# Ten short products from a 128x64 tile of ones in place of five wide ones from a 128x384 region, at the start of an attention and feed-forward kernel

## Chip, core and metric

The kernel runs on one core of a Trainium2 chip. The metric is the device time of one execution in microseconds; the kernel before takes 919.75 us, the median of 10 runs that lie between 919.09 and 921.16 us.

## What is computed

The reference has two blocks. In the first, queries and keys of 32 heads (4 batches of 8, 768 positions, 64 numbers each) are hashed: the sign of six projections gives each position a bucket, and attention counts only keys in the query's own bucket. The second block is a feed-forward layer over 3072 tokens with a gate of erf and softplus.

```python
q_bits = (np.einsum('bhsd,dk->bhsk', q, proj) > 0).astype(np.int64)
k_bits = (np.einsum('bhsd,dk->bhsk', k, proj) > 0).astype(np.int64)
mask = q_bucket[:, :, :, None] == k_bucket[:, :, None, :]
scores = np.where(mask, scale * np.matmul(q, k.transpose(0, 1, 3, 2)), -1e9)
attn = softmax(scores)          # over the keys
x = attn @ v                    # laid out as 3072 tokens x 512
h = x @ w_in                    # 512 -> 2048
out = (h * erf(softplus(h))) @ w_out
```

Nothing that the change touches enters the output: the products it edits multiply ones by ones, and no instruction reads their results.

## The kernel before

All matmuls are on float32 data, except those that carry the mask, which are bfloat16. A float32 matmul stands in the profile as two MATMUL instructions ("passes" below), each with its own weight load (LDWEIGHTS, the row PEld).

**Attention.** The 32 heads are worked as 16 pairs; the two heads of a pair sit in partitions 0 to 63 and 64 to 127. `fetch` loads one pair: queries and keys transposed to 128x768, and the values. For pair 0 it is called with `quick=True`: queries and keys come in two halves of 384 columns. The first halves go out first, q from SP's queue and k from ACT's queue; then SP's queue sends the second halves, k before q, and then the values. Each load is two DMAs, one for each head.

For pair 0 the bits are made by a short sequence that is written out by hand, ahead of the planned order:

1. the constant products (L779 to L786), which are the subject of the change;
2. for each half in turn, `hash_bits` (L369): two matmuls 128x64 by 128x384, q into partitions 0 to 63 and k into 64 to 127 of one PSUM tile (so the passes for q and for k run side by side);
3. `take_bits` (L409) for that half: `sign_bits` on ACT (L386), `spread_bits` twice on DVE (L397), `double_bits` on DVE (L407). They fill the tile `both`, from which the mask is multiplied.

`hash_bits` reads `proj_sb`, which DVE fills from a small DMA (`proj_in`, L251, copies L255).

Everything after this is put in order by `arrange` (L118), which plans with costs written in the kernel: each engine gets its instructions in the planned order. The plan does not contain the constant products or the bits of pair 0. It begins on PE with two `plain` score products (q by k, without mask, `st<-q,k`, L550), then `score` adds the mask part (`st<-both`, L550), ACT takes the exponential (L568), DVE adds the exponentials up (`sum_keys`, L619), and `weigh` multiplies them by the values (`av`, L631). The bits of every later pair go a longer way: `bits_of` on PE (L812), sign on ACT (L821), one multiplication on DVE (L831), out to DRAM from POOL's queue (`bd<-sg`, L841), and back into `both` from POOL's queue (`both<-bd`, L850). For pair 1 this happens while pair 0 is being scored. SP's queue fetches the inputs of the next pairs; POOL's queue fetches feed-forward weights (`raw`), which ACT and DVE convert beside the attention.

**Feed-forward.** Seven products in place of eight for each block of 2x2 (sums made by DVE ahead of and behind them), in stages with the erf gate on ACT and DVE between two sets of products.

**The names that matter here.** `ones` is a constant tile 128x64, filled by DVE at L247; it serves the row sums of the attention later (`divisor`, L666). `w_sum` is a large tile that the feed-forward fills much later; before, its first 384 columns are filled with ones at L248 and serve as `warm`. `bank("...")` (L299) takes a tile of 128x512 from a PSUM pool with a single buffer: each call is a new tile in the same place.

```python
    WARM = 5
    nc.vector.memset(ones, 1.0)
    nc.vector.memset(w_sum[:, 0, 0, 0:HS], 1.0)
    warm = w_sum[:, 0, 0, 0:HS]
```

Of the kernel before, what the change touches and what calls it, by code (L numbers as in the profile page):

```python
# [63 lines left out]
P = 128  # L64
# [129 lines left out]
def kernel(  # L194
# [11 lines left out]
    nc = tc.nc  # L206
    B, H, S, D = v.shape
# [5 lines left out]
    HS = S // 2  # L213
# [15 lines left out]
    small = ctx.enter_context(tc.tile_pool(name="small", bufs=3))  # L229
    QR = 32  # L230
    QB = QR // 2
    WARM = 5
    proj_sb = const.tile([P, 2 * QR], F32, name="proj_sb")
    weight = const.tile([P, 2], F32, name="weight")
    proj_q = const.tile([P, QR], F32, name="proj_q")
# [1 line left out]
    ones = const.tile([P, D], F32, name="ones")  # L237
# [5 lines left out]
    w_sum = const.tile([P, 3, 2, FH], F32, name="w_sum")  # L243
# [1 line left out]
    blocks = []  # L245
    stats = const.tile([P, 2, NPAIR, 2], F32, name="stats")
    nc.vector.memset(ones, 1.0)  # L247
    nc.vector.memset(w_sum[:, 0, 0, 0:HS], 1.0)  # L248
    warm = w_sum[:, 0, 0, 0:HS]
    proj_in = const.tile([P, 2 * NBIT], F32, name="proj_in")  # L250
    nc.gpsimd.dma_start(out=proj_in, in_=proj2)  # L251
    nc.vector.memset(proj_sb, 0.0)
    for ab in range(2):
        rows = slice(ab * D, ab * D + D)
        nc.vector.tensor_copy(  # L255
            out=proj_sb[rows, ab * QR : ab * QR + NBIT],
# [5 lines left out]
    for c, (end, factor) in enumerate(  # L262
# [12 lines left out]
            out=steps[:, c : c + 1],  # L275
# [9 lines left out]
    for ab in range(2):  # L285
        rows = slice(ab * D, ab * D + D)
        nc.vector.tensor_copy(
            out=proj_q[rows, ab * QB : ab * QB + NBIT],
# [10 lines left out]
    def bank(name):  # L299
        return misc.tile([P, 512], F32, name=name, tag="bank")  # L300
# [45 lines left out]
    def fetch(i, load, quick=False):  # L346
        d = dict(
            q=load.tile([P, S], F32, name="q", tag="q"),
            k=load.tile([P, S], F32, name="k", tag="k"),
            v=load.tile([P, NC, P], F32, name="v", tag="v"),  # L350
        )
        b, j = divmod(i, JP)
        parts = ((0, "q"), (0, "k"), (1, "k"), (1, "q")) if quick else ((None, "q"), (None, "k"))
        for half, what in parts:
            cols = slice(0, S) if half is None else slice(half * HS, half * HS + HS)
            queue = nc.scalar if quick and what == "k" and half == 0 else nc.sync
            for ab in range(2):
                queue.dma_start(  # L358
                    out=d[what][ab * D : ab * D + D, cols],
                    in_=qkT[2 * i + ab, "qk".index(what) * D : "qk".index(what) * D + D, cols],  # L360
                )
        for ab in range(2):
            nc.sync.dma_start(  # L363
                out=d["v"][:, :, ab * D : ab * D + D],
                in_=v[b, 2 * j + ab].rearrange("(c p) d -> p c d", p=P),
            )
        return d
# [48 lines left out]
    def attention():  # L416
        NS = NPAIR * 4
        with (
# [357 lines left out]
                pairs[i] = fetch(i, load)  # L776

            pairs[0] = fetch(0, load, quick=True)
            for n in range(WARM):  # L779
                nc.tensor.matmul(  # L780
                    out=bank("warm")[:, 0 : 2 * P],
                    lhsT=warm[:, 0:P],
                    rhs=warm[:, P:HS],
                    start=True,
                    stop=True,
                )  # L786
# [917 lines left out]
    with tc.manual_schedule():  # L1704
        late = attention()
        feed_forward(judge, late)
# [57 lines left out]
```

## Time and profile before

| what | us |
|---|---|
| median of 10 runs | 919.75 |
| the profiled execution, its own time | 920.35 |
| its span in the trace | 918.5 |
| PE busy | 905.5 |
| DVE busy | 819.2 |
| ACT busy | 768.1 |
| ones filled by DVE (L247), start and duration | 0.82, 0.11 |
| w_sum filled by DVE (L248), start and duration | 0.96, 0.38 |
| first constant product, start | 1.39 |
| first pass of the bits of pair 0, start | 7.66 |
| first mask product of pair 0, start | 12.57 |
| first exponential, start | 12.96 |

The profiled execution's own time is 1.85 us more than its span, and 0.6 us more than the median of the runs. "Busy" of PE counts a pass from its start to its modelled end, and passes overlap in the pipeline, so a row's duration is longer than the distance from one pass to the next. In the timeline a line gives start, duration, engine, line of code, operation and tile, and at its end the idle time before it with what ended that. In an answer about one tile, the three numbers after the count are the shortest, median and longest duration in nanoseconds.

### The profile page before, as it was taken

Reading aid. Unit: us, or ns where it says so; the run is one execution under the profiler, and the core shown is the slowest. Engines: PE = TensorE matmul, PEld = TensorE weight load, DVE = VectorE, ACT = ScalarE, POOL = GpSimd, SP = SyncE. Lnnn points to the kernel's source line nnn. Section 1 sums busy time; section 2 is a strip of 40 time slices with the busy share of each in tenths; the row PEclk is TensorE's granted clock in tenths of the full one; section 3 lists DMA queues with packets and bytes.
Section 4 is the critical chain, followed back from the end, with each engine's and each line's share of the span. In section 5 each row is a group of like instructions: output and inputs, shape, how many; then the busy total and the mean of one; then the engine's idle time right before and its main releaser. Section 6 shows DMA issues by size and latency. Waiting matters only on the chain.

```text
span 918.5 us, 13120 instructions
## 1 busy us (share of the span) xinstructions
PE 905.5 (99%) x5006; PEld 659.2 (72%) x5006; DVE 819.2 (89%) x1020; ACT 768.1 (84%) x1002; POOL 46.8 (5%) x83
## 2 busy tenths in 40 slices
PE   9999999999999999999999999999999999999996
PEld 4444444444444478888888888888888888888885
DVE  4899999999899979899999799998999889988995
ACT  5888887788887749999988998899989988899891
POOL 1211111111111000000000000000000000000000
PEclk9999999999999999999999999999999999999998
DMA  8455576655673131102022012211221120011211
GB/s 205 118 154 160 157 185 192 184 150 154 177 197 108 59 121 64 46 9 95 12 74 76 35 46 72 78 35 46 70 81 35 35 81 35 35 35 46 69 35 49
DMA packets 62966, 83.05 MB, mean 90 GB/s; under 512 B 34174, under 2 KB 47342, under 8 KB 62896
## 3 DMA queue, kind: packets, MB, share of 16 engines
q1 hardware_dynamic: 56672, 64.08, 24.0%
q0 software_dynamic: 6064, 17.86, 6.0%
q8 instruction: 41, 0.67, 0.3%
q14 instruction: 29, 0.24, 0.1%
q10 hardware_dynamic: 160, 0.20, 0.1%
HBM read 64.71 MB, written 17.40 MB: 89 GB/s over the span
## 4 chain that ended last, share of the span: by engine, by line
PE 93%; DVE 2%; DMA 2%; SPq 1%; ACT 1%; issue 0%; POOL 0%; DVEq 0%; POOLq 0%; ACTq 0%
PE M L1323 31%; PE X L1183 28%; PE st L550 16%; PE av L631 13%; PE M L1183 3%; PE z_ps L666 1%; PE bits L812 1%; SPq L358 1%; DMA v<-in_v_dram 1%; DMA raw<-in_w_in_dram 1%; DVE e L1237 0%; DVE h L1265 0%; SPq L363 0%; DMA both<-bd 0%; DVE S L1280 0%
## 5 line engine op out<-in xcount | busy, mean ns | idle before, releaser
L1250 DVE SCALAR_TENSOR_TENSOR e<-w,e 128x1024 f32<-128x1024 f32 x144 | 173.3, 1219 | 5.8 <-ACT w L1246 3.0
L568 ACT ACTIVATE e_all<-st 128x768 f32<-128x768 f32 x192 | 151.2, 813 | 14.0 <-PE st L550 13.9
L1246 ACT ACTIVATE w<-w,cq 128x1024 f32<-128x1024 f32 x144 | 160.6, 1143 | 1.9
L550 PE MATMUL st<-q,k 64*128 64x384 f32 x768 | 156.0, 485 | 0.0
L1323 PE MATMUL M<-w_out_sb,h 128*128 128x256 f32 x576 | 140.2, 379 | 0.4 <-DVE h L1265 0.4
L631 PE MATMUL av<-e_all,v 128*64 128x385 f32 (+1 forms) x768 | 131.1, 490 | 0.0
L1183 PE MATMUL X<-x,w_in_sb 128*128 128x256 f32 x512 | 121.1, 379 | 0.0
L1323 PEld LDWEIGHTS M<-w_out_sb,h 128*128 128x128 f32 x576 | 109.3, 190 | 15.9 <-DVE h L1265 1.1
L1183 PEld LDWEIGHTS X<-x,w_in_sb 128*128 128x128 f32 x512 | 97.0, 190 | 13.8 <-ACT h L1201 0.6
L631 PEld LDWEIGHTS av<-e_all,v 128*64 128x64 f32 x768 | 52.3, 136 | 67.5 <-issue 65.7
L550 PEld LDWEIGHTS st<-q,k 64*128 64x128 f32 x768 | 68.7, 189 | 35.6 <-issue 34.9
L1323 PE MATMUL M<-wt,S 128*128 128x256 f32 x384 | 93.4, 379 | 0.4 <-DVE S L1280 0.4
L1183 PE MATMUL X<-x_sum,w_sum 128*128 128x256 f32 x344 | 81.7, 380 | 1.8 <-ACT h L1201 1.8
L1323 PEld LDWEIGHTS M<-wt,S 128*128 128x128 f32 x384 | 72.9, 190 | 10.7 <-DVE S L1280 0.8
L1183 PEld LDWEIGHTS X<-x_sum,w_sum 128*128 128x128 f32 x344 | 65.0, 190 | 12.0 <-ACT h L1201 3.3
L1201 ACT COPY h<-X 128x512 f32<-128x512 f32 x85 | 49.1, 577 | 22.3 <-PE X L1183 21.4
L1227 DVE SCALAR_TENSOR_TENSOR w<-w,e 128x1024 f32<-128x1024 f32 x48 | 58.4, 1220 | 9.7 <-ACT w L1222 9.7
L550 PE MATMUL st<-both 64*128 64x384 bf16 x384 | 63.2, 324 | 0.5 <-DMA both<-bd 0.3
L1265 DVE TENSOR_TENSOR h<-h,e 128x1024 f32<-128x1024 f32 x48 | 58.0, 1220 | 5.8 <-ACT e L1261 5.5
L1241 ACT ACTIVATE w<-e 128x1024 f32<-128x1024 f32 x48 | 50.4, 1050 | 13.2 <-DVE e L1237 13.0
L1237 DVE TENSOR_TENSOR e<-e,w 128x1024 f32<-128x1024 f32 x48 | 57.4, 1217 | 2.7 <-ACT e L1233 2.6
L1205 DVE TENSOR_TENSOR h<-X,h 128x512 f32<-128x512 f32 x65 | 44.8, 689 | 16.4 <-PE X L1183 15.4
(133 smaller groups left out, 1377.6 us busy)
## 6 DMA issues: line engine op xcount, KB each, us to landing
wt<-wt SPq DMA_DIRECT2D x24, 768.0 KB, 4.3
raw<-in_w_out_dram POOLq DMA_DIRECT2D x16, 512.0 KB, 4.0
raw<-in_w_in_dram POOLq DMA_DIRECT2D x14, 512.0 KB, 4.3
v<-in_v_dram SPq DMA_DIRECT2D x32, 192.0 KB, 4.8
xs<-x SPq DMA_DIRECT2D x16, 384.0 KB, 2.6
q<-in_qkT_dram SPq DMA_DIRECT2D x30, 192.0 KB, 4.3
k<-in_qkT_dram SPq DMA_DIRECT2D x30, 192.0 KB, 4.9
r<-rd SPq DMA_DIRECT2D x30, 192.0 KB, 3.4
```

Source lines behind the costliest of these rows:

```text
L550: nc.tensor.matmul(out=st[:, ab, 0:HS], lhsT=d["k" + src][rows, keys], rhs=d["q" + src][rows, cols], start=(part == 0), stop=(part == 1),)
L568: nc.scalar.activation(out=e[:, :, 0:HS], in_=st[:, :, 0:HS], func=AF.Exp, scale=scale)
L631: nc.tensor.matmul(out=d["av"][rows, 0:w], lhsT=d["v"][:, g * GC + c, rows], rhs=e[:, ab, 0:w], start=(g == 0 and c == 0), stop=(g == 1 an ...
L1183: nc.tensor.matmul(out=d[where][:, u, :], lhsT=a[:, kc, f : f + P], rhs=b[:, kc, :], start=(first and u == 0 and kc == 0), stop=(last and ...
L1201: nc.scalar.copy(out=quarter(p, q), in_=st[p][where])
L1227: nc.vector.scalar_tensor_tensor(out=w, in0=w, scalar=-1.0, in1=st[p]["e", v], op0=ALU.add, op1=ALU.subtract)
L1237: nc.vector.tensor_tensor(out=s, in0=s, in1=st[p].pop(("w", v)), op=ALU.subtract)
L1241: nc.scalar.activation(out=z, in_=st[p]["s", v], func=AF.Square)
L1246: nc.scalar.activation(out=q, in_=z, func=AF.Square, bias=cq[:, j : j + 1])
L1250: nc.vector.scalar_tensor_tensor(out=s, in0=st[p].pop(("q", v, j)), scalar=ERF_Q[j][1], in1=s, op0=ALU.add, op1=ALU.mult,)
L1265: nc.vector.tensor_tensor(out=h, in0=h, in1=st[p].pop(("s", v)), op=ALU.mult)
L1323: nc.tensor.matmul(out=banks[name][:, sub, :], lhsT=a[:, u, sub * P : (sub + 1) * P], rhs=b[:, u, :], start=(c == 0 and k == 0), stop=(c = ...
```

## The change

The products go from five to ten. Each one now has a stationary operand of 64 columns (`ones` itself) and a moving operand of 128 columns, which is one column of `ones` read 128 times over (a step of zero), where it had 128 and 256. They write 64 partitions by 128 columns in place of 128 by 256. The PSUM tile is taken once, ahead of the loop, and all ten write to the same place in it; before, each of the five took a new tile. The fill of 384 columns of `w_sum` goes; the products wait for the fill of `ones` (64 columns), which stands first on DVE in both versions.

```diff
-    WARM = 5
+    WARM = 10
...
     nc.vector.memset(ones, 1.0)
-    nc.vector.memset(w_sum[:, 0, 0, 0:HS], 1.0)
-    warm = w_sum[:, 0, 0, 0:HS]
...
             pairs[0] = fetch(0, load, quick=True)
+            warm = bank("warm")
             for n in range(WARM):
                 nc.tensor.matmul(
-                    out=bank("warm")[:, 0 : 2 * P],
-                    lhsT=warm[:, 0:P],
-                    rhs=warm[:, P:HS],
+                    out=warm[0:D, 0:P],
+                    lhsT=ones,
+                    rhs=ones[:, 0:1].broadcast_to([P, P]),
                     start=True,
                     stop=True,
                 )
```

## Prediction

> **What bounds the kernel now.** First the page: busy times, then the chain that ended last.
>
> ```profile
> PE 905.5 (99%) x5006; PEld 659.2 (72%) x5006; DVE 819.2 (89%) x1020; ACT 768.1 (84%) x1002; POOL 46.8 (5%) x83
> ...
> PE 93%; DVE 2%; DMA 2%; SPq 1%; ACT 1%; issue 0%; POOL 0%; DVEq 0%; POOLq 0%; ACTq 0%
> ```
>
> PE is busy throughout and carries the chain. What comes earlier in the first 13 us therefore comes off the end, unless PE later waits for something that has not moved. The edit lies wholly in this stretch, so next the timeline of its start:
>
> ```profile
> 0.82 0.11 DVE L247 MEMSET ones<- 128x64 f32 x1 [0.82 <-PEq L1744]
> 0.96 0.38 DVE L248 MEMSET w_sum<- 128x384 f32 x1
> ...
> 1.39 0.50 PEld L780 LDWEIGHTS warm<-w_sum 128*128 128x128 f32 x2 [1.39 <-DVE w_sum L248]
> ...
> 2.67 0.50 PEld L780 LDWEIGHTS warm<-w_sum 128*128 128x128 f32 x2 [0.78 <-PE warm L780]
> ...
> 4.02 0.35 DVE L255 COPY proj_sb<-proj_in 64x6 f32<-64x6 f32 x2 [2.49 <-DMA proj_in<-in_proj_dram]
> ...
> 7.66 0.90 PE L373 MATMUL bits<-q,proj_sb 128*64 128x384 f32 x1
> ...
> 8.36 0.85 PE L373 MATMUL bits<-q,proj_sb 128*64 128x384 f32 x1
> ...
> 9.64 0.85 PE L373 MATMUL bits<-q,proj_sb 128*64 128x384 f32 x1
> ...
> 10.57 0.58 ACT L386 ACTIVATE both<-bits,sgn 128x384 bf16<-128x384 f32 x1 [0.70 <-PE bits L373]
> ...
> 12.57 0.65 PE L550 MATMUL st<-both 64*128 64x384 bf16 x6
> ```
>
> Each of the five products starts 1.28 us after the last; its weight load waits for the product before (0.78 us idle each time), because each takes the one PSUM buffer anew. Only at 7.66 do the bits begin, though their inputs were there: `proj_sb` at 4.37 (4.02 + 0.35), the first halves of q and k at 4.98 (the trace's last landing). So the products themselves hold up the kernel.
>
> The answer for tile `bits` shows the second thing, PE's clock:
>
> ```profile
> L373 PE MATMUL bits<-q,proj_sb x4: 847/847/903, 7.7 to 9.6; 128*64 128x384 f32 x4
> ...
> L812 PE MATMUL bits<-q,proj_q x4: 486/498/510, 18.8 to 19.1; 128*32 128x384 f32 x4
> ```
>
> Passes over the same 384 columns take 847 ns at 8 us and 498 at 19; start to start they are 0.64 us apart in L373 (9.64 - 9.00) and, in the attention's `av` rows, 0.32. So PE runs at half speed at first. (The granted clock in the view by stretches reads 1.00 there, but nothing is recorded before the first change.) In the single records two score passes are 0.64 apart until 11.87 and the next 0.38: full speed came at about 12.0, that is 4.3 us after the unbroken work began at 7.66. Six us of spaced products, which stream 0.85 of every 1.28 us (67%), had not brought it.
>
> **The change part by part.**
>
> *The fill removed.* The products wait for `ones`, filled at 0.93, not for `w_sum`, filled at 1.34. With the 0.05 us between fill and first load (1.39 - 1.34) they start at 0.99: 0.40 earlier. The other early DVE work gains nothing, since the copies wait for `proj_in` until 4.02. The first reuse of the PSUM bank (`z_ps`, 29.8) comes long after.
>
> *The products.* At half speed a pass of 128 columns takes 0.64 x 128/384 = 0.213 us. A 64-column weight load costs 0.06 when it stands exposed (8.36 - 7.66 - 0.64). Ten products are 20 passes: 0.99 + 0.06 + 20 x 0.213 = 5.31. The trace does not show such a pass. Below, full speed would halve it, but the bits then wait for inputs until 5.0. Above, each weight load stays exposed: 20 x 0.27 = 5.5, end 6.5. I take the lower pass cost: at 12.89 a weight load of 187 ns under a pass of 0.16 delayed the next pass by nothing. The broadcast read has no row either; from no loss (as any column read) to twice the pass (8.5 us, end 9.6). I take no loss, as the `av` rows read their 385 columns at the same pace as the score rows their 384, whatever the source.
>
> The Trainium skill speaks against short passes ("TensorE: Matmul & The Clock Gate", "Back-to-back issue gap"): with its weight load a 128-column matmul costs 81 ns where the stream alone takes 56. By that ratio the products would end at 7.2 and about 0.8 us of the gain below would go.
>
> *The waits removed.* One tile for all ten products means no turn of the buffer. Score products already write one PSUM tile repeatedly on PE with no wait (L550's waits name exponentials and DMAs, none PE).
>
> *The first half of the bits* starts at 5.3 in place of 7.66. Next late is the second half's q: its last load is issued at 4.20 and lands at 6.75; PE takes four waits 0.13 apart, so q starts about 6.9 and k 7.05. Had that cover not been there, 0.3 us more would be won.
>
> *The clock.* Dense work from 0.99 and 4.3 us more gives full speed at 5.3, if these half-wide products count as the bits did. Then the first half takes 0.06 + 2 x 0.32 = 0.70 and hides before 6.9; the second ends at 7.05 + 0.70 = 7.75, before 10.29 (9.65 + 0.64). ACT follows 0.28 later (10.57 - 10.29), at 8.03; from there to the mask's weights it was 12.25 - 10.57 = 1.68 through ACT and DVE: 9.71, first mask product 9.75. The plain scores (four passes of 0.32, ending about 9.3) hide beneath; before, at half speed, they ended at 12.57 and set that time. The front moves 12.57 - 9.75 = 2.8 us.
>
> By the Trainium skill (same page, "The HAM clock gate") the gate opens at the end of the first fully busy window of 3.4 us that runs freely. That gives an estimate of 4.4 to 7.9 for the release; at the late end about 0.3 us of the 2.8 goes. This trace's one release, 4.3 us after dense work began, fits.
>
> *What has not moved.* Pair 1's mask goes out and back through DRAM:
>
> ```profile
> PEld L550 <- DMA both<-bd: 0.6, 1, 0.6
> ```
>
> PE already waits 0.6 us for it at 26.65. The store `bd<-sg`, issued at 21.21, lands in 1.9 us with DMA nearly idle (share 0.12 from 20 to 25). Moved 2.8 earlier it meets pair 2's loads (share 1.2 from 18 to 20), whose issue by SP depends on nothing that moved. The next such store, at 31.57 among traffic, took 3.1. So the loss lies between 0 and 1.2 us and goes wholly into PE's wait. I take 0.6: the 3.1 row also had a weight load ahead of it in POOL's own queue, which the moved one has not. Otherwise PE, ACT and DVE move together; pair 1's loads land by 13.5, before their use.
>
> **Sum.** 2.8 - 0.6 = 2.2 us: 920.35 becomes 918.15 for the profiled execution. It lies 0.6 above the median of the runs, so the median becomes 917.55; I say **917.5**.
>
> **Rivals.**
>
> A, the forecast: dense products bring full speed before the second half of the bits. 916.3 to 918.3 (loss 0 to 1.2, clock a little late).
>
> B: products that fill 64 of 128 columns do not count, and the clock comes 4.3 us after the bits begin, or after their short gap at 6.9. The second half then ends at 7.05 + 0.06 + 1.28 = 8.39, the plain scores run at half speed until 9.6 or beyond, and the mask product starts at 10.45 to 11.25: 1.3 to 2.1 won, 0.4 given back: 918.0 to 918.9, or 918.4. For it: the row's 64 columns use half the array. Against: nothing here shows what the clock counts; the bits' 64-column passes came as side-by-side pairs.
>
> C, slower than before: the framework keeps a wait between products that overwrite one tile. Each costs what L780's row shows around its passes, 1.28 - 0.16 - 0.85 = 0.27, plus 0.06 and 2 x 0.213: 0.75. The tenth starts at 0.99 + 9 x 0.75 = 7.74, the bits at 8.4 (+0.06 + 0.43 + 0.15): 0.7 later than 7.66, 920.4. It decides once a product costs over 0.67 us ((7.66 - 0.99)/10). For it: DVE and ACT rows do wait for their own engine; against: L550 on PE does not.
>
> D: the early start is used up later, in waits for DMA that stays in place: 919.7. For it, the 0.6 wait above; against, PE's 99%, and few PE waits after 30 us.
>
> **Chances.** A 0.55, B 0.25, C 0.08, D 0.08, worse mishaps (such as the doubled pass) 0.04. About 0.2%, or 1.84 us, is what a measurement of this kernel can tell from no change, so faster means under 917.91. A lies there four times in five (0.44) and B one in five (0.05): faster 0.49. Slower by as much needs over 921.59: the mishaps and a bad C or D, 0.06. Within: 0.45. The range, 916.2 to 919.9, takes in A, B and D and leaves out C.
>
> **What would show it.** Right: products from about 0.99, 0.21 us from pass to pass, none waiting for PE; bits from about 5.3, the second half at 6.9, its passes near 500 ns rather than 847; the first mask product near 9.75; PE's wait for `both<-bd` grown from 0.6 to about 1.2. B: 847 ns in all bits rows. C: 0.75 us between products with waits named PE. D: the first exponential 2 to 3 us earlier and the last matmul not. The forecast fails first if short passes cost more than 0.29 us, since the products then outlast the second half's landing.

## The result and the profile after

| what | before | after |
|---|---|---|
| median, us (runs) | 919.47 (28) | 923.58 (8), from 922.36 to 924.71 |
| ratio, 95% interval | | 1.0042 [1.0033, 1.0051] |
| the profiled execution, us | 920.35 | 922.51 |
| its span, us | 918.5 | 920.7 |

The change makes the kernel 0.42% slower, by about 4 us, where 2.2 us were forecast as won. (The kernel before was run again beside it; hence 919.47 and not 919.75.) The profiled execution is 2.16 us longer than that of before.

The page first: busy times, the granted clock (PEclk, how much of its full speed TensorE's clock was allowed, in tenths) in 40 slices, and the chain that ended last.

```profile
PE 904.9 (98%) x5016; PEld 661.6 (72%) x5016; DVE 819.2 (89%) x1019; ACT 767.8 (83%) x1002; POOL 46.5 (5%) x83
...
PEclk9899999999999999999999999999999999999999
...
PE 95%; DVE 2%; DMA 1%; ACT 1%; SPq 0%; issue 0%; POOL 0%; DVEq 0%; ACTq 0%; POOLq 0%
```

PE still carries the end, and it is busy 0.6 us less in a span that is 2.2 us longer. So it waits more. The 8 in the second slice (23 to 46 us) is new (before, only the last slice has an 8): the clock was lower there for a while.

The timeline of the start shows the front as it was meant to be:

```profile
0.99 4.42 PE L779 MATMUL warm<-ones 128*64 128x128 f32 x20 [0.99 <-DVE ones L247]
...
5.24 0.49 PE L371 MATMUL bits<-q,proj_sb 128*64 128x384 f32 x1
...
6.74 0.51 PE L371 MATMUL bits<-q,proj_sb 128*64 128x384 f32 x1 [0.62 <-DMA q<-in_qkT_dram]
...
9.02 0.65 PE L548 MATMUL st<-both 64*128 64x384 bf16 x6
...
17.66 0.54 POOL L840 DMA_DIRECT2D bd<-sg  x1 [13.81 <-DVE sg L830]
```

Products at 0.99 without a wait, bits at 5.24, their second half behind its load at 6.74, and the first mask product at 9.02 where it was at 12.57: 3.55 us earlier. The store `bd<-sg` follows at 17.66, also 3.55 earlier (21.21 before). Thus far everything moved together. The waits from 18 to 32 us (engine, line, what was waited for, then the sum, how often, the longest) show where it stops:

```profile
ACT e_all L566 <- PE st L548: 5.9, 3, 4.9
POOL both L849 <- DMA bd<-sg: 5.1, 1, 5.1
...
PE st L548 <- DMA both<-bd: 4.0, 2, 3.5
```

The same two rows before:

```profile
POOL both L850 <- DMA bd<-sg: 2.0, 1, 2.0
...
PE st L550 <- DMA both<-bd: 0.3, 1, 0.3
```

POOL waits 5.1 us for the store (2.0 before), and PE 4.0 us for the loads back (0.3 before). The timeline of that place:

```profile
22.75 1.11 SPq L356 DMA_DIRECT2D q<-in_qkT_dram  x2
...
23.29 1.14 POOL L849 DMA_DIRECT2D both<-bd  x2 [5.08 <-DMA bd<-sg]
...
26.19 0.48 PE L548 MATMUL st<-both 64*128 64x384 bf16 x1 [3.54 <-DMA both<-bd]
...
27.12 0.50 PE L548 MATMUL st<-both 64*128 64x384 bf16 x1 [0.46 <-DMA both<-bd]
...
28.88 1.62 PE L548 MATMUL st<-q,k 64*128 64x384 f32 x4
```

The row of before for the second mask product of pair 1:

```profile
26.66 0.33 PE L550 MATMUL st<-both 64*128 64x384 bf16 x1 [0.30 <-DMA both<-bd]
```

The store lands at 22.61 (23.12 before): of 3.55 us, 0.5 is left. The loads back go out at 23.29, beside pair 3's loads, which SP's queue now sends at 22.75 (26.29 before). The second lands after 3.21 us (2.24 before), and the second mask product of pair 1 runs at 27.12, 0.46 us later than before. And the passes behind it take 1.62 us for four, where they take 0.81 elsewhere. The view by stretches tells why (busy time and instructions of PE, PEld, DVE, ACT, POOL; then granted clock, DMA share, GB/s):

```profile
22.00:24.00 2.00, 0.64 (x4) 0.03 (x2) 1.97 (x3) 2.00 (x3) 0.71 (x2) 1.00 0.00 1
24.00:26.00 2.00, 0.00 (x0) 0.00 (x0) 1.97 (x3) 0.06 (x1) 2.00 (x3) 0.91 0.94 255
26.00:28.00 2.00, 1.35 (x5) 0.81 (x7) 1.33 (x2) 0.00 (x0) 0.32 (x1) 0.50 1.03 229
28.00:30.00 2.00, 2.00 (x10) 1.27 (x8) 0.00 (x0) 0.81 (x1) 0.00 (x0) 0.50 0.50 193
30.00:32.00 2.00, 2.00 (x8) 0.79 (x4) 0.00 (x0) 0.81 (x1) 0.00 (x0) 0.50 0.00 0
32.00:34.00 2.00, 2.00 (x21) 0.78 (x22) 0.24 (x1) 1.66 (x4) 0.00 (x0) 0.88 0.00 0
```

PE idles from 22.64 to 26.19, the granted clock falls to half at 25.65, and it stays there until 32.47, while PE, from 27.12 without a pause, works on pair 1's scores. The first `av` of pair 1 starts at 33.33 instead of 30.29 (before, then after):

```profile
30.29 1.19 PE L631 MATMUL av<-e_all,v 128*64 128x384 f32 x6
...
33.33 0.87 PE L629 MATMUL av<-e_all,v 128*64 128x384 f32 x4
```

The account of the path is therefore: front 3.55 earlier, all of it and 0.46 more lost to the transfers, and 3.04 - 0.46 = 2.58 us lost to the clock. The 3.04 us stay to the end: the last matmul starts at 913.41 (910.32 before), 3.09 us later. The two profiled executions differ by only 2.16 us, because the stretch behind the last matmul took 6.9 us after and 7.8 before; the medians differ by 4.1, and the 1 us between that and 3.09 stays unexplained.

Why does the store take 4.95 us where it took 1.90? The DMA view from 18.8 to 19.4 us, more than a microsecond after its issue (queue, packets, MB, share of 16 engines; q1 carries SP's loads, q0 POOL's transfers; the share adds up the packets' own times and can pass 100%):

```profile
q1 hardware_dynamic: 404, 0.11, 129.9%
```

Not one packet of the store is among 404, nearly all of them 256-byte rows of pair 2's values. From 20.4 to 20.8 it comes through:

```profile
q0 software_dynamic: 21, 0.06, 58.5%
q1 hardware_dynamic: 146, 0.03, 55.3%
```

The Trainium skill ("DMA: Bandwidth & Descriptors", "Queues, rings and completion order") has each DMA engine take packets from its queues in turn. By that rule the store would be among them, at an estimate from about 18.8 on (in e9_sp_waits below, from the same queue, its packets begin then). This trace shows its first packet at 20.2 and the others as the loads ahead of it run out. The measurement decides.

### The profile page after: what moved, and what is told of

The parts are those of the page before. It is cut to its first block, busy times and chain, and to the rows that moved or that the text cites. A ratio compares the mean times of both kernels' runs of the same rounds, so it can differ in the third digit from the quotient of the medians.

```text
span 920.7 us, 13139 instructions
## 1 busy us (share of the span) xinstructions
PE 904.9 (98%) x5016; PEld 661.6 (72%) x5016; DVE 819.2 (89%) x1019; ACT 767.8 (83%) x1002; POOL 46.5 (5%) x83
## 4 chain that ended last, share of the span: by engine, by line
PE 95%; DVE 2%; DMA 1%; ACT 1%; SPq 0%; issue 0%; POOL 0%; DVEq 0%; ACTq 0%; POOLq 0%
PE M L1322 31%; PE X L1182 28%; PE st L548 17%; PE av L629 14%; PE M L1182 3%; PE z_ps L664 1%; PE bits L811 1%; ACT e_all L566 1%; DMA bd<-sg 1%; DVE e L1236 0%; SPq L356 0%; DMA both<-bd 0%; DMA q<-in_qkT_dram 0%; DVE h L1264 0%; DVE S L1279 0%
## 5 line engine op out<-in xcount | busy, mean ns | idle before, releaser
L566 ACT ACTIVATE e_all<-st 128x768 f32<-128x768 f32 x192 | 151.1, 812 | 19.7 <-PE st L548 18.8
```

The lines of the kernel that those rows point to most:

```text
L566: nc.scalar.activation(out=e[:, :, 0:HS], in_=st[:, :, 0:HS], func=AF.Exp, scale=scale)
```

## The experiments

The theory: the front's gain is real; it is lost because pair 2's loads, which hardly moved (issued from 10.85 to 14.49, before from 11.11 to 15.07), hold up pair 1's store and so the mask, and the idle time then takes the clock down. Rivals: the clock alone is to blame; the fault is in the products (half-wide ones, or one tile); something later takes the time back. Each kernel was timed beside the kernel before. The column "pair 1" is the first `av` of pair 1 in the profiled execution against 30.29 before; a profile is one execution, so it can stand a microsecond or two off the median.

| kernel | median | before | ratio, 95% interval | pair 1 |
|---|---|---|---|---|
| e1_fill | 921.68 | 919.80 | 1.0014 [1.0001, 1.0028] | +1.65 |
| e10_fill7 | 920.21 | 919.67 | 1.0008 [0.9998, 1.0018] | +1.22 |
| e2_hold_all | 916.14 | 919.80 | 0.9954 [0.9937, 0.9971] | -3.61 |
| e3_hold_before | 918.92 | 919.23 | 0.9994 [0.9986, 1.0003] | -1.03 |
| e2a_hold_store | 917.97 | 919.23 | 0.9982 [0.9973, 0.9990] | -2.27 |
| e9_sp_waits | 918.70 | 919.67 | 0.9989 [0.9981, 0.9998] | -0.92 |
| e7_hold_v | 918.61 | 919.23 | 0.9988 [0.9974, 1.0002] | +1.85 |
| e4_wide_dense | 922.48 | 919.80 | 1.0024 [1.0012, 1.0036] | +4.36 |
| e5_warm22 | 918.56 | 919.80 | 0.9990 [0.9972, 1.0008] | -0.11 |
| e8_k_on_act | 916.74 | 919.23 | 0.9967 [0.9955, 0.9979] | -3.77 |

### What the clock costs: e1_fill and e10_fill7

The changed kernel with filler products in `score`, in the place where PE waits. Their results are read by nobody. The diff is that of e1_fill; e10_fill7 has 7 for 5.

```diff
+                if (n, c) == (4, 0):
+                    keep_busy(5)
...
+            def keep_busy(count):
+                fill = bank("fill")
+                for n in range(count):
+                    nc.tensor.matmul(
+                        out=fill[0:D, 0:HS],
+                        lhsT=ones,
+                        rhs=ones[:, 0:1].broadcast_to([P, HS]),
+                        start=True,
+                        stop=True,
+                    )
```

> The changed kernel with five more products of ones (64 columns by 384, about 3.2 us at full speed, results unread) on PE just ahead of pair 1's first mask product, where PE stood idle for 3.5 us. Nothing else moves. Theory 1 (PE idles because pair 1's mask comes late from DRAM, and the idle stretch drops the clock to half from 25.6 to 32.5): the clock stays full, the av products of pair 1 start about 2.6 us earlier, 921.0 against 923.6 for the changed kernel. Rival (the half clock does not come from the idle stretch but from the shape or density of the ten products or from the early release): clock still drops, 923.6.

Five fillers end at 26.18, and PE idles 1.21 and 0.60 us in place of 3.54 and 0.46. The clock holds in the profiled execution, but by the mean granted clocks not in every one: the twelve runs spread from 919.19 to 923.51, the five with a mean of 0.998 or more from 919.19 to 921.38, the four with 0.996 from 921.99 to 922.78. (0.997 alone tells nothing: the profiled execution of before has it, with no fall ahead of its end.) Too few fillers, and so an answer only in part.

> The changed kernel with seven filler products (64 columns by 384 rows, results not used) instead of five in the place where TensorE waits for pair 1's bits: some 4.5 us, about the whole idle time of 3.54 and 0.46 us. Theory (the wait costs the whole early start and 0.5 us more, and the fall of the clock after it costs 2.6 us on top): the clock stays full behind the fillers in nearly every execution, TensorE waits under 0.6 us, pair 1's end is between 30.3 and 32, and the time is 919.5 to 921. Rival (the clock's fall in the profile is not what made the changed kernel slow over its executions): the time stays at 922 or more although the clock holds. The fillers may themselves end up to 1 us late, which would put it at the upper end.

Seven cover the wait. The clock holds:

```profile
26.00:28.00 2.00, 1.72 (x8) 0.51 (x8) 1.35 (x2) 0.00 (x0) 0.82 (x2) 1.00 0.91 195
28.00:30.00 2.00, 2.00 (x17) 1.41 (x16) 0.00 (x0) 1.10 (x2) 0.00 (x0) 1.00 0.56 221
```

Full clock (1.00) where the changed kernel shows 0.50; all twelve runs have a mean clock of 0.997 to 0.999 (0.993 to 0.995 in all ten executions of the changed kernel that are on record) and the time is 920.21. So the clock's fall costs about 1.0042 - 1.0008 = 0.34%, some 3.1 us, and the wait alone leaves the kernel about where it was before. The trace of the changed kernel had 2.58 for it; what the other half microsecond is stays open.

### Take the loads out of the store's way: e2_hold_all and e3_hold_before

Pair 2's loads are issued behind pair 1's store and loads back, all on SP's queue. The order on PE, DVE and ACT stays. e2_hold_all does it to the changed kernel, e3_hold_before to the one before. The loads back take the same `queue` as the store.

```diff
-                nc.gpsimd.dma_start(out=bd.rearrange("n a r c -> (n a r) c"), in_=sg)
+                queue = nc.sync if i == 1 else nc.gpsimd
+                queue.dma_start(out=bd.rearrange("n a r c -> (n a r) c"), in_=sg)
...
-            for each in arrange(ops, {}):
+            plan = arrange(ops, {})
+            late_pair = next(each for each in plan if each.name == ("start_pair", 2))
+            plan.remove(late_pair)
+            at = next(n for n, each in enumerate(plan) if each.name == ("place_bits", 1))
+            plan.insert(at + 1, late_pair)
+            for each in plan:
```

> The changed kernel with pair 1's store of bits and its two loads back issued from SP's queue, and pair 2's loads put behind them on that queue; the order on PE, ACT and DVE is that of the changed kernel. Theory 1 (the store and the loads back met pair 2's loads): store and loads back take 2 us and 2.3 us, PE has no idle stretch and the clock stays full, and the whole early start of 3.5 us is kept: 915.5 to 917, depending on whether pair 2's q and k come in time for their bits. Rival (the loss is in the products' shape or the clock by itself): 923.6. A second rival (the DRAM round trip is slow early in the kernel whatever runs beside it): store still about 5 us, 922 or more.

```profile
17.51 0.33 SPq L841 DMA_DIRECT2D bd<-sg  x1
19.16 0.67 SPq L851 DMA_DIRECT2D both<-bd  x2
```

The store, issued at 17.51, lands at 19.11, and the loads back go out at 19.16 where they left at 23.29. PE has no wait there any more, the clock never falls, pair 1 is 3.61 us ahead of before, and the time falls by 3.66. Nothing later takes it back. This kernel beats both.

> The kernel before (five spaced wide products, late start) with the same move as in the run that held all of pair 2's loads: pair 1's store and loads back on SP's queue, pair 2's loads behind them. Theory 1 (the move is worth only the wait that it takes away, and before there were just 0.3 to 0.6 us of it): 919.2 to 919.6 against 919.8. Rival (the gain of 3.7 us in that run came from the move itself and not from the early start): 916 to 917.

Without the edit the same hold goes with pair 1 earlier by 1.03 us and a time shorter by 0.3 us, which can't be told from nothing. Of the 1.03 us, 0.68 were there before the hold could act: in this execution the clock was released at 10.60 (11.98 before) and the first mask product stood at 11.89 (12.57). So the gain of e2_hold_all is the edit's, let through. Against e3_hold_before it is 0.9954/0.9994 = 0.9960, or 3.7 us.

### Which transfer, and queue or order: e2a, e9, e7

e2a_hold_store moves the store alone to SP's queue, ahead of pair 2's loads (`leave_bits` for `place_bits` in the diff above, and no change to the loads back).

> The changed kernel with only the store of pair 1's bits moved to SP's queue ahead of pair 2's loads; the two loads back stay on POOL's queue and so run beside pair 2's q and k loads. Theory 1 (each of the two hops is lengthened by the loads that it meets): the store lands by 19.2, the loads back leave at about 19.8 and 20.4 and take 3.3 to 3.8 us each, PE waits 1 to 2 us, the clock stays full: 917.3 to 918.5, between the run with both hops ahead (916.1) and before. Rival (only the store matters): 916.1.

The store lands at 19.21 (issued 17.60). The loads back now run beside pair 2's queries and keys and take 3.17 and 3.89 us; PE waits 0.34 and 0.88 us. The store gives most of the gain, the loads back the rest.

e9_sp_waits leaves all three on POOL's queue and only makes SP wait, with a small transfer that reads `sg`; the plan is that of e2a_hold_store:

```diff
+                if i == 2:
+                    mark = dram.tile([1, 64], BF16, name="mark", tag="mark", bufs=1)
+                    nc.sync.dma_start(out=mark, in_=sg[D : D + 1, 0:64])
```

> The changed kernel, but the loads of pair 2 (on SP's queue) come behind pair 1's store of the skewed bits: SP first moves one small tile that reads sg (so it waits for the same result as the store), and then issues pair 2's loads. The store itself and the two loads back stay on POOL's queue. The small transfer is extra work and is not the reference's. Theory (the store is late because pair 2's loads are in the DMA engines ahead of it, whichever queue it comes from): the store lands within about 2 us of its issue at 17.6, at 19.5 to 20, instead of 22.61; the loads back then run beside pair 2's loads, and TensorE waits at most 1.5 us for them, as where the store alone was moved to SP's queue; no fall of the clock; 917 to 918.6. Rival (the gain in the held versions came from the change of queue, POOL's against SP's, and not from the order against pair 2's loads): the store still takes 3.5 us or more, TensorE waits 2 us or more, and the time is 920.5 to 923.6.

From 18.8 to 19.4, the stretch in which the changed kernel moved none of the store:

```profile
q1 hardware_dynamic: 20, 0.06, 55.2%
q0 software_dynamic: 44, 0.08, 43.4%
```

44 of its 48 packets. It lands at 19.58 from POOL's queue, 1.92 us after its issue, as before the change. So it is the order against pair 2's loads and not the queue, which settles what e2_hold_all, where both changed, had left open. The loads back were mispriced: they stand behind pair 2's loads, take 4.00 and 4.87 us, and PE waits 1.75 and 1.03 us for them, more than the 1.5 expected; the time is 0.1 above the range for that reason.

e7_hold_v sends only pair 2's values later, behind pair 3's keys: `fetch` puts their two loads into a list, and `start_pair(3)` issues them.

```diff
-    def fetch(i, load, quick=False):
+    def fetch(i, load, quick=False, later=None):
...
+                if i == 3:
+                    later.pop()()
```

> The changed kernel with one edit on SP's queue: the two loads of pair 2's values go out behind pair 3's keys in place of ahead of them; store and loads back stay on POOL's queue. Theory 1 (the store lands when the loads that were queued ahead of it are done, whenever it is issued): pair 2's k is then the last, it landed at 21.1 in the changed kernel, so the store lands at about 21.2 in place of 22.6, the loads back leave 1.4 us earlier, PE waits about 2 us and the clock stays full: 918.3 to 920. Rival (the store is slowed by the 256-byte rows of the values only): store in about 2.5 us, 916.5 to 917.

The store still takes 3.92 us (17.89 to 21.81). Pair 2's queries and keys, ahead of it, have all landed at 20.34. Of its 48 packets, 30 run from 18.8 to 19.4, beside 30 of SP's queue, and 45 have started by 20.0; the last three start at 20.73 to 21.34, when SP's queue moves nothing, and why they are so late isn't shown. PE waits twice, 1.84 and 1.88 us, and the clock, which was expected to stay full, falls:

```profile
24.00:26.00 2.00, 0.32 (x1) 0.09 (x1) 1.97 (x3) 0.29 (x1) 1.52 (x2) 1.00 0.87 209
26.00:28.00 2.00, 1.09 (x5) 0.91 (x7) 1.56 (x2) 0.00 (x0) 0.00 (x0) 0.69 0.95 219
28.00:30.00 2.00, 2.00 (x10) 1.10 (x7) 0.00 (x0) 0.81 (x1) 0.00 (x0) 0.50 1.04 288
30.00:32.00 2.00, 2.00 (x24) 0.90 (x20) 0.00 (x0) 1.67 (x3) 0.00 (x0) 0.96 0.84 147
```

Half speed for one stretch of 3.41 us. This execution (921.28) is among the slowest of the kernel, though; most of its twelve runs lie from 916.84 to 919.83. The values are a part of what stands ahead of the store, not all of it.

### Which part of the change: e4_wide_dense and e5_warm22

e4_wide_dense is the kernel before with nothing but one PSUM tile for its five wide products:

```diff
+            wide = bank("warm")
...
-                    out=bank("warm")[:, 0 : 2 * P],
+                    out=wide[:, 0 : 2 * P],
```

> The kernel before with one edit: the one PSUM tile for the five wide products is taken once, so that they do not wait for each other; the shape (128 columns by 256), the tile of w_sum and its fill stay. Theory 1: what matters is when the front starts, not the shape; dense products bring full speed at about 5, the second half of the bits starts at 6.8, the same late mask of pair 1 and the same idle stretch with half clock: 923.5. Rival (the shape or the operand of the short products is to blame): early front without the loss, 916 to 919.

That alone is slower than before (0.24% of the 0.42%): mask at 9.33, PE idle for 4.35 and 0.56 us, clock at half from 27.06 to 33.89. So an early front does harm without short products, 64 columns or `ones`; here it comes from taking away the waits between the products. It was expected at 923.5 and took 922.48. Whether the shape has a part in the rest isn't shown: the intervals of the two kernels (1.0012 to 1.0036, and 1.0033 to 1.0051) overlap.

e5_warm22 is the changed kernel with `WARM = 22`, so that the front is early by a part only.

> The changed kernel with 22 short products in place of 10. They end at about 8.2 (24 more passes of 0.11 to 0.14 us at full speed), so the front comes about 2.4 us later than in the changed kernel and 1.2 us earlier than before. Theory 1 (a collision in time): the store of pair 1's bits leaves at about 20, when pair 2's loads are nearly done, PE waits less than 2 us, the clock stays full: 918.3 to 919.5, faster than the changed kernel although PE starts later. Rival (early clock release or the products themselves): 923.6 plus 2.

The mask starts at 11.29, 1.28 us earlier than before, and the store lands at 23.16 although issued 1.29 us earlier (19.93): pair 1 keeps 0.11. PE idles 1.13 us. Eight of the twelve runs lie from 917.72 to 918.65 at a mean clock of 0.998 or 0.999, four from 921.44 to 923.16 at 0.994 to 0.996: medians of 918.38 and 922.13. One kernel, with and without a fall of the clock, 3.7 us apart; that the four had such a fall is read from their clocks alone, since the profiled execution is one of the eight. The kernel before has such runs too: of the 30 beside this one, the four with a mean clock of 0.995 or 0.996 took 922.90 to 923.80.

### A second try on the front: e8_k_on_act

e2_hold_all with the second half of pair 0's keys on ACT's queue, so that SP's queue sends q sooner.

```diff
-            queue = nc.scalar if quick and what == "k" and half == 0 else nc.sync
+            queue = nc.scalar if quick and what == "k" else nc.sync
```

> The run with both hops held ahead of pair 2's loads, and in addition the second half of pair 0's k loaded from ACT's queue in place of SP's, so that SP issues the second half of q 1.25 us earlier. Theory 1 (with the wait for the mask gone, what bounds the front is the landing of q's second half at 6.75): it lands near 5.6, the second half of the bits starts about 1 us earlier, 915.1 to 915.6 against 916.1. Rival (something else is due at the same time, such as the next DRAM trip or DVE's weights at 5.9): 916.1.

The second half of q is issued 1.3 us sooner (2.26 and 2.90) and lands at 5.97 and 6.78 (6.36 and 6.72 in e2_hold_all). The last of it comes no sooner, and the time (0.9967) isn't better than that of e2_hold_all (0.9954); their intervals overlap. The time at which loads are issued did not set when the last one landed.

## Why the prediction was wrong

**Right: the products, the waits, the clock's release, the bits.** They start at 0.99, go at 0.213 us from pass to pass (forecast 0.213), and end just before the bits at 5.24 (5.31). The Trainium skill's higher price for short matmuls ("TensorE: Matmul & The Clock Gate", "Back-to-back issue gap"), weighed in the prediction, does not show in these passes, which ran at half clock. No wait stands between products to one tile, so rival C falls. Full speed comes at 5.17 (5.3). That it came so close is luck: in the eight other traces with these short products it came between 4.15 and 6.99. Little hangs on it: with 6.99 the first mask product of e1_fill stood at 9.17, against 9.02. (The prediction's estimate from the Trainium skill, 4.4 to 7.9, should have ended at 0.99 + 2 x 3.41 = 7.8, and the 4.15 of e9_sp_waits lies below it.) The second half of the bits runs at full speed:

```profile
L371 PE MATMUL bits<-q,proj_sb x4: 486/486/507, 5.2 to 7.1; 128*64 128x384 f32 x4
```

Medians of 486 ns against 847: rival B falls. Half-wide dense products bring the clock, as do the wide ones of e4_wide_dense (6.58).

**Right in kind, too small in size: the front.** Forecast 2.8, measured 3.55, because ACT took the signs of the second half at 7.74 instead of 8.03, and the mask's weights followed them by 0.96 us (8.70), not by the 1.68 taken over from before; the mask product then started 0.32 us after its weights, where 0.04 was forecast.

**The step that failed: "What has not moved".** It said: "the loss lies between 0 and 1.2 us and goes wholly into PE's wait. I take 0.6". The loss was 3.55 + 0.46 = 4.01 us. The upper end came from another store's row (3.1 us at 31.57), as if a store had a latency that some traffic lengthens. (The 0.6 us that PE was said to wait already is the row of its weight loads; PE's own idle time there was 0.30. And with a loss of 0 the sum gives 919.75 - 2.8 = 916.95, not the 916.3 at which case A begins.) The runs show another thing: it lands when the loads ahead of it have run out. Its landing hardly knows its issue:

| kernel | store issued | landed |
|---|---|---|
| after | 17.66 | 22.61 |
| e1_fill | 17.82 | 23.20 |
| e5_warm22 | 19.93 | 23.16 |
| before | 21.21 | 23.12 |
| e7_hold_v, values behind it | 17.89 | 21.81 |
| e9_sp_waits, loads behind it | 17.66 | 19.58 |

The trace of before could have said so. Its row of DMA shares from 17 to 22 us, in tenths and in slices of 0.125 us:

```profile
DMA  9979999999999999999999964401111111111000
```

The same row of the changed kernel, with the store now in it:

```profile
DMA  9699599999997999999999999999984302112011
```

Before, the engines are full until about 19.9, with loads that the change does not edit. A store moved to 18 would come out behind them, not 1.9 us after its issue; I read their mean share over two-microsecond stretches and took a latency from elsewhere. The loads back were left out altogether: pair 3's loads, which do move with the front (26.29 to 22.75), now run beside them, and that is the last microsecond (3.21 against 2.24).

**What no case had: the clock's second fall.** The prediction used the half-speed clock at the start and never asked what a long idle time in the middle does to it. PE's 3.54 us of idle cost 6.83 us at half speed, 2.6 us of the path in the trace and 3.1 by e10_fill7. Rival D was the right kind, an early start used up in a wait for DMA that stays in place. But it ended at "nothing gained", and without the clock it would have been right to a microsecond (e10_fill7: +0.54). With it the result lies 3.7 us above the range.

## What to carry to other kernels

Before a stage is moved forward, follow the transfers that it issues: in the trace of before, find when the loads already queued at the new time run out, and count the landing from there, not from the latency of a similar transfer. If TensorE will then idle for some 3 us out of 3.4, in one wait or in two, add the clock's fall to the price. An early start that loses time can still be good work: let the small transfers on the path go ahead of the bulk loads (0.9954 here) instead of undoing it.

## What was not expected of the hardware

- A store from POOL's queue did not share the DMA engines with loads already queued from SP's: 0 of 48 packets in a stretch in which, with the loads behind it, 44 ran. With queries and keys alone ahead of it (e7_hold_v), 30 ran in that stretch, while those loads were landing. Whether the store waits on each DMA engine by itself isn't shown, as the traces don't tell the engines apart.
- After one idle time of 3.54 us the clock was at half for 6.83 us, after 4.35 for 6.83 (e4_wide_dense), after 1.84 and 1.88 with one pass between them for 3.41 (e7_hold_v). After 1.75 and 1.03 us (e9_sp_waits), and after 1.2 or less, the profiled executions show no fall. The changes of the clock lie 20.48, 6.83 and 3.41 us apart, multiples of 3.413. The Trainium skill has it so ("TensorE: Matmul & The Clock Gate", "What's actually happening"): a window of 3413 ns that runs freely, and half clock after an idle one. Counted in stretches of 3.41 us from a change of the clock, the idle times fall into order. Here are two of the changed kernel, then two of e7_hold_v, then the one of e9_sp_waits that holds its longer wait (PE's busy time is the number behind the comma, the granted clock the third from the end):

```profile
22.24:25.65 3.41, 0.40 (x4) 0.00 (x0) 3.38 (x4) 1.82 (x3) 2.36 (x3) 1.00 0.46 128
25.65:29.06 3.41, 2.42 (x10) 1.51 (x12) 1.68 (x2) 0.12 (x1) 0.67 (x2) 0.50 0.99 269
...
23.34:26.75 3.41, 0.32 (x1) 0.09 (x1) 3.34 (x4) 0.95 (x2) 2.18 (x3) 1.00 0.74 172
26.75:30.16 3.41, 3.25 (x13) 2.17 (x15) 0.84 (x1) 0.81 (x1) 0.00 (x0) 0.50 1.02 267
...
21.22:24.63 3.41, 1.66 (x11) 0.54 (x8) 3.31 (x5) 2.84 (x4) 2.18 (x3) 1.00 1.19 227
```

The clock fell after stretches with 0.40 and 0.32 us of PE's work, and not after one with 1.66; it stayed at half after one with 2.42 and came back after one with 3.25. So two short waits do what one long one does when they fall into one stretch. Where between 0.40 and 1.66 us the limit lies isn't shown, nor why 1.13 us of idle go with a lower clock in four of twelve runs of e5_warm22.

- Products with 0.43 us of pause in each 1.28 us did not release the clock in 6 us; dense ones did in 3.2 to 6.0 us after they began (at 4.15 to 6.99 in the profiled executions), whether 64 or 128 columns wide.
